# Two early input loads moved from SP's queue to ACT's queue in an attention-and-experts kernel

## The chip, the cores and the metric

The kernel runs on one core of a Trainium2 chip. The metric is device time in microseconds (us) of one execution, lower is better. Executions of one kernel here lie within about 2 us of each other; a few were 1 to 4% longer at a lower granted clock, the share of its full rate that PE was given ("slow"), and these are left out of every mean below. Each kernel also left one profile. A profile's times count from the start of its span; the span is 1.7 to 1.9 us shorter than the device time of the same run. In the profiles PE is the matmul engine, DVE, ACT and POOL are the vector, scalar and GpSimd engines, SP only issues transfers here, and a "q" behind a name marks the engine's instruction sequencer. A line of a profile begins with its start and its length in us; a bracket at its end tells how long the engine was idle before it and what ended that.

## The reference, cut to what matters

Four batches, eight heads, 768 steps, head size 48. A gated linear attention keeps a 48x48 state per head; its output goes through a mixture of four experts.

```python
f = 1.0 / (1.0 + np.exp(-f_logit))
for t in range(S):
    state = f[:, :, t, :, None] * state + np.einsum('bhd,bhe->bhde', k[:, :, t], v[:, :, t])
    y[:, :, t] = np.einsum('bhd,bhde->bhe', q[:, :, t], state)
...
p = domain_probs / (domain_probs.sum(-1, keepdims=True) + 1e-09)
for e in range(E):
    h = np.maximum(x @ w1[e], 0.0)
    out += p[:, e:e + 1] * (h @ w2[e])
```

The kernel computes the attention in six chunks of 128 steps. Only the first chunk has no expert work to hide under: until its four batches have passed attention, PE has nothing large to multiply.

## The kernel before

The order of all steps is planned in Python before anything is emitted, and each engine then runs its steps in that fixed order. The first chunk's 16 loads of 192 KB (letter: gate logits f, keys k, queries q, values v; digit: batch) are planned in this order, all from SP's queue:

```python
for i, x in enumerate("f0 k0 q0 f1 k1 q1 f2 f3 k2 q2 v0 k3 q3 v1 v2 v3".split()):
    add_load(0, x[0], int(x[1]), 1, -1000 + i)
...
def load(c, nm, b, n):
    ins[c, nm, b] = nc.sync.dma_start(out=tl(nm, c, b // 2)[:, hh(b, n), :],
                                      in_=srcs[nm][c, :, b * H:(b + n) * H, :])
```

The expert weights come through POOL's software queue, with a cast to bf16. The first of them waits for the last keys of chunk 0, and stands in POOL's order behind three key products:

```python
def load_w(i, e, which):
    w, r = (w1_sb, w1_r) if which == 1 else (w2_sb, w2_r)
    ins["w", i] = nc.gpsimd.dma_start(out=w[:, e], in_=r[e])
    if i == 0:
        after(ins["w", 0], ins[0, "k", B - 1])
```

In the first chunk, gaps of PE's plan are filled with matmuls on a constant tile, whose results nobody reads ("fillers"):

```python
for o in done:
    for _ in range(o.pad):
        nc.tensor.matmul(out=spare[:, 0:256], lhsT=busy[:, 0:128], rhs=busy, start=True, stop=True)
    o.emit(o.engine)
```

## Time and profile before

| | before |
|---|---|
| median of the first 3 runs, us | 305.67 (305.66 to 306.22) |
| span of the profile, us | 303.5 |
| PE busy | 97% |
| batch 0's logits land | 3.72 |
| last copy of chunk 0's activations ends | 22.92 |
| first expert weights land | 22.99 |
| first expert matmul starts | 23.04 |

To read it: PE is full from 23 us on, so the span is the start of the first expert matmul plus a constant. That constant is 303.5 - 23.04 = 280.5 us here. The whole question is what sets that start. Two paths end there within 0.07 us: the attention of the first chunk, ending in the copy, and the weights. The prediction shows the lines.

### The profile page before, as it was taken

Reading aid. Unit: us, or ns where it says so; the run is one execution under the profiler, and the core shown is the slowest. Engines: PE = TensorE matmul, PEld = TensorE weight load, DVE = VectorE, ACT = ScalarE, POOL = GpSimd, SP = SyncE. Lnnn points to the kernel's source line nnn. Section 1 sums busy time; section 2 is a strip of 40 time slices with the busy share of each in tenths; the row PEclk is TensorE's granted clock in tenths of the full one; section 3 lists DMA queues with packets and bytes.
Section 4 is the critical chain, followed back from the end, with each engine's and each line's share of the span. In section 5 each row is a group of like instructions: output and inputs, shape, how many; then the busy total and the mean of one; then the engine's idle time right before and its main releaser. Section 6 shows DMA issues by size and latency. Waiting matters only on the chain.

```text
span 303.5 us, 5499 instructions
## 1 busy us (share of the span) xinstructions
PE 294.5 (97%) x2104; PEld 170.5 (56%) x2135; DVE 137.8 (45%) x272; ACT 170.7 (56%) x295; POOL 95.7 (32%) x157
## 2 busy tenths in 40 slices
PE   7899999999999999999999999999999999999995
PEld 5665555567775655455555555555555555555552
DVE  6684013788853764516555344544423443201223
ACT  5767654957865444676356475345476444475430
POOL 4585200408656237423426243522432000000000
PEclk9999999999999999999999999999999999999999
DMA  7999999955993589776997877301322201100002
GB/s 156 204 185 208 208 206 190 225 90 91 215 208 82 111 165 181 170 144 120 189 178 136 213 142 151 51 13 37 92 59 51 48 14 41 73 5 2 0 0 104
DMA packets 137210, 36.08 MB, mean 119 GB/s; under 512 B 128480, under 2 KB 135648, under 8 KB 137184
## 3 DMA queue, kind: packets, MB, share of 16 engines
q1 hardware_dynamic: 131424, 29.45, 48.8%
q0 software_dynamic: 5760, 6.29, 12.5%
q8 instruction: 16, 0.26, 0.4%
q14 instruction: 10, 0.08, 0.1%
HBM read 31.51 MB, written 4.72 MB: 119 GB/s over the span
## 4 chain that ended last, share of the span: by engine, by line
PE 90%; DMA 4%; DVE 2%; POOL 1%; issue 1%; ACT 1%; DVEq 0%; ACTq 0%; POOLq 0%
PE ps_m L356 40%; PE ps_m L344 40%; DMA w_sb<-in_moe_w_dram 3%; PE ps_t L300 2%; PE ps_t L255 1%; PE ps_t L315 1%; PE ps_t L321 1%; PE ps_t L311 1%; PE ps_t L285 1%; DMA f<-in_f_logit_dram 1%; POOL qk L276 1%; PE ps_m L551 1%; DVE qk L276 1%; DVE o L363 0%; DVE AT L304 0%
## 5 line engine op out<-in xcount | busy, mean ns | idle before, releaser
L352 ACT ACTIVATE h<-ps_m 128x512 bf16<-128x512 f32 (+1 forms) x171 | 98.4, 578 | 102.7 <-PE ps_m L344 92.5
L356 PE MATMUL ps_m<-w_sb,h 128*128 128x384 bf16 x768 | 153.0, 326 | 0.2
L344 PE MATMUL ps_m<-xT,w_sb 128*128 128x512 bf16 (+1 forms) x593 | 150.4, 362 | 1.9 <-DVE o L367 0.3
L356 PEld LDWEIGHTS <-h 128*128 128x128 bf16 x768 | 72.5, 98 | 57.4
L363 DVE SCALAR_TENSOR_TENSOR o<-ps_m,pn,o 128x384 f32<-128x384 f32 x72 | 44.4, 617 | 97.2 <-PE ps_m L356 89.8
L344 PEld LDWEIGHTS <-w_sb 128*128 128x128 bf16 x624 | 59.8, 98 | 46.9 <-issue 0.7
L276 POOL TENSOR_TENSOR qk<-q,e 128x384 bf16<-128x384 f32 x19 | 22.8, 1203 | 66.7 <-ACT e L262 66.2
L304 DVE TENSOR_TENSOR AT<-ps_t,mask 128x512 bf16<-128x512 f32 x48 | 31.1, 685 | 19.3 <-PE ps_t L300 19.2
L335 POOL TENSOR_TENSOR Sf<-Sf,egs 48x192 f32<-48x192 f32 x40 | 20.4, 510 | 47.5 <-DVE Sf L328 45.5
L350 DVE TENSOR_SCALAR h<-ps_m 128x512 bf16<-128x512 f32 (+1 forms) x37 | 20.7, 573 | 22.0 <-PE ps_m L344 19.7
L276 POOL TENSOR_TENSOR qk<-k,e 128x384 bf16<-128x384 f32 x20 | 21.3, 1064 | 20.3 <-ACT e L264 13.0
L262 ACT ACTIVATE e<-ps_t 128x384 f32<-128x384 f32 x24 | 20.7, 864 | 4.6 <-PE ps_t L255 2.4
L328 DVE TENSOR_TENSOR Sf<-Sf,ps_t 48x192 f32<-48x192 f32 x40 | 14.0, 350 | 9.4 <-PE ps_t L321 8.7
L336 POOL CAST sb<-Sf 48x192 bf16<-48x192 f32 x40 | 13.6, 339 | 2.6
L551 PE MATMUL ps_m<-busy 128*128 128x256 bf16 x71 | 13.1, 332 | 1.3 <-DVE busy L140 1.3
L365 ACT ACTIVATE o<-ps_m,pn 128x384 f32<-128x384 f32 x20 | 11.6, 581 | 3.9 <-PE ps_m L356 3.1
L264 ACT ACTIVATE e<-ps_t 128x384 f32<-128x384 f32 x24 | 13.0, 541 | 0.0
L218 DVE CAST yb<-ps_t 128x384 bf16<-128x384 f32 x16 | 8.9, 556 | 7.3 <-PE ps_t L315 6.3
L247 ACT ACTIVATE ex<-f 128x768 f32<-128x768 f32 (+1 forms) x14 | 10.5, 747 | 3.0 <-DMA f<-in_f_logit_dram 3.0
L315 PE MATMUL ps_t<-vb,AT 128*128 128x48 bf16 x192 | 11.4, 184 | 0.7 <-DVE vb L218 0.7
L315 PEld LDWEIGHTS <-AT 128*128 128x128 bf16 x192 | 9.8, 97 | 2.8 <-issue 0.9
L251 ACT ACTIVATE gp<-ex 128x768 bf16<-128x768 f32 (+1 forms) x14 | 10.5, 751 | 0.4
(50 smaller groups left out, 142.6 us busy)
## 6 DMA issues: line engine op xcount, KB each, us to landing
w_sb<-in_moe_w_dram POOLq DMA_DIRECT2D x8, 768.0 KB, 18.6
out_dram<-o SPq DMA_DIRECT2D x24, 192.0 KB, 1.9
f<-in_f_logit_dram SPq DMA_DIRECT2D x10, 384.0 KB, 4.2
k<-in_k_dram SPq DMA_DIRECT2D x10, 384.0 KB, 5.3
q<-in_q_dram SPq DMA_DIRECT2D x10, 384.0 KB, 5.3
v<-in_v_dram SPq DMA_DIRECT2D x10, 384.0 KB, 5.5
f<-in_f_logit_dram SPq DMA_DIRECT2D x4, 192.0 KB, 3.8
k<-in_k_dram SPq DMA_DIRECT2D x4, 192.0 KB, 3.9
```

Source lines behind the costliest of these rows:

```text
L262: nc.scalar.activation(out=e[:, 0].rearrange("t (d h) -> t h d", d=D), in_=cs[:, 0:HD].rearrange("t (i r d) -> t r i d", r=2, d=D), func=A ...
L276: engines[eng].tensor_tensor(out=tl("qk", c, b)[:, j, :, 0:D].rearrange("t (i r) d -> t i r d", r=2), in0=tl("qk"[j], c, b // 2)[:, hh(b), ...
L304: nc.vector.tensor_tensor(out=tl("AT", c, b)[:, r].rearrange("s i t -> s (i t)"), in0=tl("A", c, b, r).rearrange("s i t -> s (i t)"), in1= ...
L315: nc.tensor.matmul(out=y[:, h * D:(h + 1) * D], lhsT=AT[:, r, i, :], rhs=vb[:, h, :], start=(c == 0), stop=True, skip_group_check=True)
L328: nc.vector.tensor_tensor(out=Sf[rows, b], in0=Sf[rows, b], in1=KV[rows, :, r, :], op=ALU.add)
L335: nc.gpsimd.tensor_tensor(out=Sf[rows, b], in0=Sf[rows, b], in1=eg, op=ALU.mult)
L344: nc.tensor.matmul(out=tl("hp", c, e, fc, n0)[:, n0:n1], lhsT=w1_sb[:, e, kk, fc * 128:(fc + 1) * 128], rhs=tl("xT", c)[:, kk, n0:n1], sta ...
L350: nc.vector.tensor_relu(out=dst, in_=src)
L352: nc.scalar.activation(out=dst, in_=src, func=AF.Relu)
L356: nc.tensor.matmul(out=tl("op", c, e, nt)[:, 0:Din], lhsT=tl("h", c, e)[:, fc, nt * T:(nt + 1) * T], rhs=w2_sb[:, e, fc, :], start=(fc == ...
L363: nc.vector.scalar_tensor_tensor(out=o, in0=op, scalar=pe, in1=o, op0=ALU.mult, op1=ALU.add)
L551: nc.tensor.matmul(out=spare[:, 0:256], lhsT=busy[:, 0:128], rhs=busy, start=True, stop=True)
```

## The change

The intent is to have two sequencers start the first loads, so that they get going sooner: batch 0's keys and batch 1's logits are issued by ACT, which waits for its first data anyway.

```diff
     def load(c, nm, b, n):
-        ins[c, nm, b] = nc.sync.dma_start(out=tl(nm, c, b // 2)[:, hh(b, n), :],
+        ins[c, nm, b] = (nc.scalar if (c, nm, b) in ((0, "k", 0), (0, "f", 1)) else nc.sync).dma_start(out=tl(nm, c, b // 2)[:, hh(b, n), :],
                                           in_=srcs[nm][c, :, b * H:(b + n) * H, :])
```

PE, DVE and POOL keep their instruction order. SP has two issues fewer; ACT has two more, behind its table load and ahead of the first exponential.

## The prediction

> **What bounds the kernel now.** I read the page from the top, then the chain of waits in order of time, then the timeline of the first 24 us and the stretches of one us for the DMA. On the page I looked at busy time first:
>
> ```profile
> span 303.5 us, 5499 instructions
> PE 294.5 (97%) x2104; PEld 170.5 (56%) x2135; DVE 137.8 (45%) x272; ACT 170.7 (56%) x295; POOL 95.7 (32%) x157
> ```
>
> PE is busy for 97% of the span, and the stretches of ten us show 9.6 to 10.0 us of PE in nearly each after 30 us. So from the first large matmul on, the time is PE's own work, and a change that touches only the first microseconds moves the end by as much as it moves that first matmul. PE's count in the first 23 us includes filler matmuls on the tile "busy", so there being busy proves nothing; the chain of waits says what counts (start, length, what):
>
> ```profile
> 0.81 2.91 DMA f<-in_f_logit_dram
> 3.74 0.53 ACT ex L247
> 4.29 0.53 ACT gp L251
> 4.87 0.48 PE ps_t L255
> 5.34 0.28 PE ps_t L258 x4
> 5.63 2.58 PE ps_m L551 x12
> 8.21 0.43 PE ps_t L285 x4
> 8.63 0.32 PE ps_t L255
> ...
> 13.60 1.31 POOL qk L276
> 14.91 8.08 DMA w_sb<-in_moe_w_dram
> ...
> 23.04 0.39 PE ps_m L344
> ```
>
> The head is thus: batch 0's gate logits land at 0.81 + 2.91 = 3.72 us, gates, cumulative sum, a fixed run of fillers, batch 1's sum, products, then the first expert weights, which land at 14.91 + 8.08 = 22.99, and the first expert matmul at 23.04. The timeline (start, length, engine, and in brackets the wait) shows a second path that ends in the same tenth of a microsecond, the last of the four transposed activations:
>
> ```profile
> 22.44 0.48 ACT L216 COPY xT<-ps_t 128x384 bf16<-128x384 bf16 x1 [0.74 <-PE ps_t L340]
> 23.03 0.55 PEld L344 LDWEIGHTS <-w_sb 128*128 128x128 bf16 x4 [0.36 <-DMA w_sb<-in_moe_w_dram]
> ```
>
> The copy ends at 22.92, the weights land at 22.99. The change can gain only if both come earlier; it loses if either comes later.
>
> The change concerns the loads, so I looked at their issues on SP's queue and at the DMA engines (last two columns of the stretches: busy share of the 16 engines, GB/s):
>
> ```profile
> 0.81 0.45 SPq L222 DMA_DIRECT2D f<-in_f_logit_dram  x1
> 1.31 0.57 SPq L222 DMA_DIRECT2D k<-in_k_dram  x1
> 1.92 0.80 SPq L222 DMA_DIRECT2D q<-in_q_dram  x1
> 2.76 0.71 SPq L222 DMA_DIRECT2D f<-in_f_logit_dram  x1
> ...
> 1.00:2.00 1.00, 0.74 (x4) 0.56 (x5) 1.00 (x7) 1.00 (x1) 0.79 (x5) 1.00 0.02 5
> 2.00:3.00 1.00, 1.00 (x7) 0.69 (x6) 0.89 (x7) 0.09 (x1) 0.93 (x4) 1.00 0.95 186
> 3.00:4.00 1.00, 1.00 (x6) 0.69 (x5) 0.89 (x2) 0.26 (x1) 0.44 (x1) 1.00 1.11 221
> ```
>
> Bytes flow from 2.0 us, and from then on the engines are full (share about 1, some 190 to 230 GB/s in most stretches up to 17 us). One load is 192 KB, so at about 205 GB/s it costs some 0.95 us. The landings, issue plus time to landing, agree: batch 0's logits 3.7, its keys 4.5, its queries 5.6, batch 1's logits 6.4, its keys 7.5 us, steps of 0.8 to 1.15 us. SP's sequencer is not what limits the loads after the very first; its issues stretch to 0.7 to 1.5 us because the engines behind them are full.
>
> **What the Trainium skill says.** (1) "DMA: Bandwidth & Descriptors", section "Issuing engines are not separate DMA queues": transfers started by several engines run on the same 16 DMA engines and interleave; starting them from more engines saves only the sequencer's time for the start. The trace agrees as far as one queue can show it: 16 full engines from 2.0 us. (2) The same page, section "Queues, rings and completion order": SP and ACT each have a ring on each DMA engine, and an engine takes turns between rings packet by packet. Before, only SP's ring held these loads, so no run yet shows the turns. (3) "Perfetto Trace Analysis", section "DVE / Act Engine Instruction": the sequencer is free for the next instruction once it has pushed one to the wait queue; so the table load on ACT (0.80 to 2.08 us here) need not hold back the issues behind it. This trace has no issue on ACT and can't confirm it. (4) The same page, section "DMA Instruction — HWDGE": descriptor generation is locked for one issue at a time. The first, undisturbed, issue took 0.45 us on SP here.
>
> **The change part by part.** *Removed from SP:* two issues, 0.57 and 0.71 us. Batch 0's queries, batch 1's keys and all later loads can be issued 0.6, then up to 1.3 us earlier. Bytes and DMA engines stay the same, and these were full, so all loads together land no earlier: gain 0. Nothing on the chain waits for those later loads either (batch 2's and 3's logits have landed when ACT comes to them at 10.40 and 11.39 with no wait shown).
>
> *Added to ACT:* two issues of 0.45 to 0.8 us, ahead of the first exponential in ACT's order. ACT stands idle from 2.08 to 3.74, "1.65" in its timeline, waiting for the logits. If the issues run beside the table load they end near 2.5; if they start behind it at 2.08, near 3.4. Either way before 3.74: cost 0.
>
> *Moved in the rings:* this is the part that counts. Before, batch 0's logits had the DMA engines alone: data about 2.0 to 3.0 us, plus 0.7 to the landing. Now batch 0's keys stand in a second ring. Case A, ACT issues during the table load, from about 0.9 us: with the generator locked in turn the keys start 0.45 us behind the logits; the logits move 0.45 us of their 0.95 us alone and the other 0.5 at half speed in 1.0 us: landing 0.5 us later, about 4.2. If the two generators run freely or ACT comes first, up to 0.9 us later, about 4.6. Case B, ACT issues only from 2.08: the keys' bytes come near 3.3 us, when the logits are through: 0. But then batch 1's logits, second in ACT's ring and sharing with SP's, end after four loads' work from about 3.3 us, so near 7.3 + 0.7 = 8.0 at worst, against 6.4 before. They were needed at 6.79 with some 0.4 to 0.6 us to spare (their gate ended at 7.86; PE started on it at 8.43 behind fillers and transposes). Cost 0 to 0.6, say 0.2.
>
> Nothing between 3.7 and 22.9 us takes up a delay of the first logits: PE is in program order, and the 12 fillers and everything behind them move as a block; POOL, DVE and ACT wait for each other and not for a clock. So the last copy of the activations moves from 22.92 to 22.92 + d, and the first expert matmul from 23.04 to about 23.04 + d - 0.07. The weights themselves should still land near 23.0: POOL issues them d later, but the DMA engines have input loads to move until 18 us, and all bytes up to the end of the first weights stay the same.
>
> Sum: case A (7 in 10) about +0.55, case B (3 in 10) about +0.15: +0.4 us. 305.67 + 0.4 = **306.1 us**.
>
> **Rivals.** *The loads flow sooner and the head gets shorter.* For it: SP is rid of 1.28 us, and the first weights wait in POOL's order behind products that need loaded keys. Against it: share about 1 from 2.0 us on, and no load but the first ended a wait on the chain. It could gain at most the 0.07 us between the two paths without moving both; I give it 0.1 to 0.3 us of gain at best, 305.4.
>
> *PE's own speed in the head.* A filler of 128x256 takes 3.17 / 14 = 0.23 us at the start and 0.71 / 5 = 0.14 us near 21 us; the row of granted clock is full throughout. PE runs slower until about 10.5 us. A longer idle gap before its first real matmul (0.44 us now, about 1 us in case A) may put the step to the fast rate later. Each us of that would cost perhaps 0.3 us more on the chain; time 306.5 to 307.
>
> *The transfer is hidden anyway.* If ACT's ring gets its turn only after SP's first load is through, nothing moves and the time is 305.7 within the scatter of the three runs (305.66 to 306.22).
>
> *Delay absorbed later.* PE waits 0.29 us near 70 us for a product on DVE; what released that is itself behind PE, so I expect 0 to 0.2 us back.
>
> **Range and chances.** Gain 0.3 and absorbed delay give the lower end, 305.4; full sharing (+0.9) with a little of the slower PE gives the upper end, 306.8. Two per cent is 6.1 us, more than any term here and nearly half of what the head from the logits' landing to the weights' issue takes (11.2 us). So within 2% with 0.985; faster by that 0.005; slower 0.01, for a disturbed order I don't see.
>
> **What the changed profile would show.** ACT's queue has two issues, near 0.9 (case A) or 2.1 us (case B). The chain's first piece ends at 4.2 to 4.6 us in case A instead of 3.72; in case B batch 1's exponential shows a wait for its logits. The DMA's share stays about 1 from 2.0 us. The 12 fillers, the later sums and the last copy of the activations move by one amount, and the first expert matmul then waits for that copy instead of the weights, which still land near 23.0. From there to the end the length is unchanged, some 280 us. The prediction is wrong if the logits land no later yet the time rises, if the weights land more than 0.3 us away from 23.0, or if the stretch behind 23 us changes length.

## The result, and the profile after

Median 305.6 us (304.81 to 316.58, six runs, one of them slow) against 305.67. Ratios here are the mean time of one kernel's fast runs over that of the other's fast runs of the same rounds, so they are not quite the ratio of the medians: 0.9992, with a 95% interval of 0.997 to 1.0013.

The profile after has a span of 304.3 us, 0.8 more than before. First the issues, in the timeline of the changed kernel (start, length, queue; lines of other work between them are left out):

```profile
0.80 0.45 SPq L222 DMA_DIRECT2D f<-in_f_logit_dram  x1
0.83 0.48 ACTq L222 DMA_DIRECT2D k<-in_k_dram  x1
1.31 0.57 SPq L222 DMA_DIRECT2D q<-in_q_dram  x1
1.34 0.70 ACTq L222 DMA_DIRECT2D f<-in_f_logit_dram  x1
...
4.41 0.52 ACT L247 ACTIVATE ex<-f 128x384 f32<-128x384 f32 x1 [2.33 <-DMA f<-in_f_logit_dram]
```

ACT issues its first load 0.03 us after SP's, during its own table load (0.80 to 2.08 us). The exponential that needs batch 0's logits waits 2.33 us for them instead of 1.65. Now the chain of waits of the changed kernel in order of time:

```profile
0.80 3.58 DMA f<-in_f_logit_dram
...
4.41 0.53 ACT ex L247
...
5.54 0.48 PE ps_t L255
...
6.30 2.58 PE ps_m L551 x12
8.88 0.43 PE ps_t L285 x4
...
14.28 1.31 POOL qk L276
15.59 8.21 DMA w_sb<-in_moe_w_dram
23.81 0.05 issue
23.85 0.39 PE ps_m L344
```

Set it against the chain in the prediction: the logits land at 4.38 instead of 3.72 (+0.66), the fillers start at 6.30 instead of 5.63 (+0.67), the last key product ahead of the weights at 14.28 instead of 13.60 (+0.68), the weights are issued at 15.59 instead of 14.91 (+0.68). The head moved as one block. The last step did not keep to that: the weights landed 0.81 us later, at 23.80, behind the last copy of the activations, which ends at 23.61:

```profile
23.13 0.48 ACT L216 COPY xT<-ps_t 128x384 bf16<-128x384 bf16 x1 [0.74 <-PE ps_t L340]
23.85 1.47 PE L344 MATMUL ps_m<-xT,w_sb 128*128 128x512 bf16 x5 [0.21 <-DMA w_sb<-in_moe_w_dram]
```

The DMA engines are at least as full as before. These are stretches of one us (the last two columns are the engines' busy share and GB/s):

```profile
1.00:2.00 1.00, 0.75 (x4) 0.56 (x5) 1.00 (x7) 1.00 (x1) 0.79 (x5) 1.00 0.03 7
2.00:3.00 1.00, 1.00 (x7) 0.69 (x6) 0.89 (x7) 0.09 (x1) 0.93 (x4) 1.00 0.96 176
3.00:4.00 1.00, 1.00 (x6) 0.69 (x5) 0.89 (x2) 0.00 (x0) 0.44 (x1) 1.00 1.28 258
```

Two queues moved no more bytes between 1 and 3 us (183 KB against 191 before), only in another order. From 3 to 6 us they moved about a tenth more (242 GB/s against 218), but from 1 to 12 us it is 192 against 187, and kernels of one queue reach 192 as well. So the profile shows a loss of 0.8 us, and the timed runs show none. The experiments ask whether the later logits really cost time, and why the clock does not show it.

### The profile page after: what moved, and what is told of

Same layout as the page of the kernel before. It is cut to its first block, busy times and chain, and to the rows that moved or that the text cites. A ratio compares the mean times of both kernels' runs of the same rounds, so it can differ in the third digit from the quotient of the medians.

```text
span 304.3 us, 5499 instructions
## 1 busy us (share of the span) xinstructions
PE 294.4 (97%) x2104; PEld 170.1 (56%) x2135; DVE 137.9 (45%) x272; ACT 170.7 (56%) x295; POOL 95.7 (31%) x157
## 4 chain that ended last, share of the span: by engine, by line
PE 90%; DMA 4%; DVE 2%; issue 1%; POOL 1%; ACT 1%; DVEq 0%; ACTq 0%; POOLq 0%
PE ps_m L356 40%; PE ps_m L344 40%; DMA w_sb<-in_moe_w_dram 3%; PE ps_t L300 2%; PE ps_t L255 1%; PE ps_t L315 1%; PE ps_t L321 1%; PE ps_t L285 1%; DMA f<-in_f_logit_dram 1%; PE ps_t L311 1%; PE ps_m L551 1%; DVE qk L276 1%; POOL qk L276 0%; DVE o L363 0%; DVE AT L304 0%
## 5 line engine op out<-in xcount | busy, mean ns | idle before, releaser
L276 POOL TENSOR_TENSOR qk<-q,e 128x384 bf16<-128x384 f32 x19 | 22.8, 1203 | 66.7 <-ACT e L262 66.2
```

Of the source, the lines that this page charges most:

```text
L276: engines[eng].tensor_tensor(out=tl("qk", c, b)[:, j, :, 0:D].rearrange("t (i r) d -> t i r d", r=2), in0=tl("qk"[j], c, b // 2)[:, hh(b), ...
```

## The experiments

Twelve runs in three sets. Each set had its own 10 or 11 fast runs of the kernel before, with means of 305.50, 305.68 and 305.27 us; with the six first runs that is 37 runs, mean 305.50, standard deviation 0.53. All profiles in one table (us):

| kernel | logits land | last copy ends | weights land | first expert matmul | span |
|---|---|---|---|---|---|
| before | 3.72 | 22.92 | 22.99 | 23.04 | 303.5 |
| changed | 4.38 | 23.61 | 23.80 | 23.85 | 304.3 |
| a1_again (changed) | 4.26 | 23.47 | 22.9 | 23.52 | 303.9 |
| a2_keys_first | 4.82 | 23.41 | 24.81 | 24.86 | 305.2 |
| a4_logits_fourth | 6.34 | 25.19 | 24.2 | 25.24 | 305.7 |
| b2_k_only_held | 3.57 | 22.57 | 22.87 | 22.92 | 303.4 |
| b1_k_only | 4.29 | 23.13 | 24.0 | 24.09 | 304.8 |
| c1_late_fill | 3.77 | 23.93 | 22.4 | 23.98 | 304.3 |
| c2_late_fill_two_queues | 4.23 | 24.81 | 22.8 | 24.86 | 305.5 |
| e1_fewer_fillers | 3.74 | 22.57 | 23.4 | 23.43 | 304.2 |
| e1_again | 3.70 | 22.52 | 22.76 | 22.80 | 303.2 |
| e2_fewer_fillers_two_queues | 4.33 | 22.99 | 23.3 | 23.30 | 304.0 |
| c1_again | 3.59 | 24.09 | 23.5 | 24.14 | 304.5 |
| c2_again | 4.21 | 24.53 | 22.4 | 24.58 | 305.3 |

In every row the first expert matmul starts right behind the later of the two columns before it. (Weights given to one decimal are issue plus the profile's rounded time to landing.)

### First set: is it the later logits, and what is it worth?

**a1_again**: the changed kernel, no edit.

> The changed kernel once more, to tell the size of its effect from the scatter. Theory 1 (the later landing of batch 0's logits is carried one to one to the end): batch 0's logits land 3.5 to 3.6 us after their issue, the first expert matmul starts near 23.85 us, and the timed ratio is 1.002 to 1.003 (+0.6 to +0.9 us). Theory 2 (the end is not tied to the head so tightly; the +0.8 us of the one profile is scatter from run to run): ratio 0.999 to 1.001.

Measured: ratio 0.999 (0.9972 to 1.0007), mean 305.21 us. The landing (4.26 us, 3.45 behind its issue) was nearly as Theory 1 said. The first expert matmul at 23.52 was later than before by 0.48 us, not by the expected 0.8, and the ratio showed no loss. By the ratio alone, Theory 2 holds. With the first set of timed runs, the changed kernel has 11 fast runs with a mean of 305.29, 0.21 below the 37 runs of before, with a standard error of 0.15 from the spread of the runs.

**a2_keys_first**: one queue, the keys ahead of the logits.

```diff
-    done = P.run()
+    done = P.run(); j = next(i for i, o in enumerate(done) if o.name == "ld k0.0"); i = next(i for i, o in enumerate(done) if o.name == "ld f0.0"); done.insert(j, done.pop(i))
```

> One queue only, as before the change, but batch 0's keys are issued on SP ahead of batch 0's logits. Theory 1: logits land near 4.4 to 4.6 us (0.7 to 0.9 later), fillers, sums, last copy and first expert matmul move by the same amount, ratio 1.002 to 1.003: the same loss as the changed kernel without a second queue. Theory 2: ratio within 0.001 of 1. Rival 3 (the second queue itself costs something): first expert matmul near 23.1 and ratio 1.000 here, unlike the changed kernel.

Measured: ratio 1.0022 (1.0004 to 1.004), as Theory 1 had it, from a landing 1.1 us later instead of the expected 0.7 to 0.9. So this order costs time with one queue as well, and Rival 3 is not needed for a loss. That the later logits are the cost is not shown by it, because in its profile, of the slowest of the six runs, the weights came last:

```profile
22.93 0.48 ACT L216 COPY xT<-ps_t 128x384 bf16<-128x384 bf16 x1 [0.73 <-PE ps_t L340]
24.86 1.47 PE L344 MATMUL ps_m<-xT,w_sb 128*128 128x512 bf16 x5 [1.42 <-DMA w_sb<-in_moe_w_dram]
```

The activations were ready at 23.41 and PE waited another 1.4 us for the weights, which took 9.4 us from issue to landing; before the change it was 8.1, in a1_again 7.5. The same 768 KB, in the same place of the program.

**a4_logits_fourth**: the same edit with "ld f0.1" as the mark, so that batch 0's logits are issued fourth.

> The suspected cause made large: batch 0's logits are issued fourth on SP, behind batch 0's keys and queries and batch 1's logits. Theory 1: they land near 6.4 us (+2.7), the first expert matmul starts near 25.6 to 25.8, the end moves by +2.6 to +2.9 us, ratio 1.0085 to 1.0095. Theory 2: later waits take up most of it, ratio under 1.004.

Measured: ratio 1.0066 (1.0048 to 1.0085), mean 307.52 against 305.50. The logits landed 2.6 us later and the end moved by 2.0 us. Theory 2's "under 1.004" is out, and Theory 1's full size (1.0085 to 1.0095) was not reached. The last copy moved by 2.27 us only: from landing to copy it took 18.85 us instead of 19.20. And by their mean span of 303.78, less 280.45, the runs of the kernel before start their expert matmuls not at 23.04 but near 23.3 on average; with the constants seen it can be 23.0 to 23.5. That suggests that many of them wait for something else already.

**b2_k_only_held**: only the keys go to ACT's queue, and ACT holds them for a POOL memset that ends near 2.3 us.

```diff
-(nc.scalar if (c, nm, b) in ((0, "k", 0), (0, "f", 1)) else nc.sync)
+(nc.scalar if (c, nm, b) == (0, "k", 0) else nc.sync)
...
-    nc.gpsimd.memset(ones, 1.0)
+    ones_set = nc.gpsimd.memset(ones, 1.0)
...
-        if (c, nm, b) == (1, "f", 0):
-            after(ins[c, nm, b], ins["w", 5])
+        if (c, nm, b) in ((0, "k", 0), (1, "f", 0)):
+            after(ins[c, nm, b], ones_set if c == 0 else ins["w", 5])
```

> Only batch 0's keys go to ACT's queue, and they wait there for a memset on POOL that ends near 2.3 us, so that their bytes come when the logits are through. Theory 1: logits land at 3.7 us as before the change, the whole head is where it was (first expert matmul near 23.05), ratio 0.999 to 1.001, although a second queue is in use. Rival 3 (the second queue itself costs): logits or the first expert matmul late by 0.3 us or more.

Measured: the logits landed at 3.57 us. The ratio, 1.0018, has an interval of 0.9979 to 1.0056 because one of its six runs took 309.07 us without being counted as slow; the other five average 305.47. (Its granted clock was 0.994, but a run of the kernel before took 305.40 at the same clock, so that does not explain it.) So the landing speaks clearly against Rival 3 and the time is inconclusive alone.

### Second set: take the weights out of the way

**b1_k_only** is b2 without the hold, one look. The edit is the first change of b2's diff.

> Only batch 0's keys on ACT's queue, not held back. If the two rings share the DMA engines from the start: batch 0's logits land at 4.2 to 4.4 us (3.6 to 3.7 when the same load was held until 2.3 us) and the last copy of the activations ends near 23.4 to 23.6 us. If not: landing at 3.7.

Measured: landing at 4.29 us; the one execution took 306.48 us. ACT's timelines behind its table load, of b2_k_only_held and, in the second fence, of b1_k_only:

```profile
2.30 0.42 ACTq L222 DMA_DIRECT2D k<-in_k_dram  x1
3.58 0.52 ACT L247 ACTIVATE ex<-f 128x384 f32<-128x384 f32 x1 [1.50 <-DMA f<-in_f_logit_dram]
```

```profile
4.30 0.52 ACT L247 ACTIVATE ex<-f 128x384 f32<-128x384 f32 x1 [2.22 <-DMA f<-in_f_logit_dram]
```

The same load on the same second queue delays the logits by 0.7 us when it is issued beside them, and not at all when issued 1.5 us later. It is the time of the issue that matters, not the queue. The last copy came at 23.13, earlier than the 23.4 to 23.6 expected; the weights, at 24.0, set the start.

**c1_late_fill** and **c2_late_fill_two_queues**: 16 more fillers ahead of the last activation transpose, in the kernel before and in the changed one.

```diff
-        for _ in range(o.pad):
+        for _ in range(o.pad + 16 * (o.name == "xt 0.3")):
```

> The kernel before with 16 more filler matmuls on PE ahead of the last activation transpose, so that the last copy of the activations ends about 1.8 us later and the landing of the first expert weights (22.9 to 24.8 us in the profiles so far) no longer sets the start of the expert matmuls. Theory A (the landing of the first weights scatters by more than a microsecond from run to run, is what most runs of the kernel before wait for, and hides a delay of the head): first expert matmul near 24.6 us, span near 305.0, ratio 1.003 to 1.005, runs within 0.7 us of each other. Theory B (the scatter is elsewhere, behind the start of the expert matmuls): the runs scatter as before, by 1.5 us or more.

> The same 16 fillers in the changed kernel; the pair with the run before it shows the change with the weights' landing out of the way. Theory A: batch 0's logits land near 4.3 us, the first expert matmul starts 0.5 to 0.65 us later than in the pair's other kernel, and the mean time is 0.4 to 0.7 us higher. Theory B (the two queues win back elsewhere what the later logits cost): the two means differ by less than 0.2 us.

Measured: c1 306.34 us (four fast runs), c2 306.79 us (six), ratios 1.0018 and 1.0033 to the kernel before; the difference of the pair is 0.45 us. In both the copy now sets the start; first c1, then c2:

```profile
23.45 0.48 ACT L216 COPY xT<-ps_t 128x384 bf16<-128x384 bf16 x1 [2.20 <-PE ps_t L340]
...
23.98 1.46 PE L344 MATMUL ps_m<-xT,w_sb 128*128 128x512 bf16 x5
```

```profile
24.33 0.48 ACT L216 COPY xT<-ps_t 128x384 bf16<-128x384 bf16 x1 [2.20 <-PE ps_t L340]
...
24.86 0.81 PE L344 MATMUL ps_m<-xT,w_sb 128*128 128x512 bf16 x2
```

The matmul lines have no wait for the weights. c1's four fast runs lie within 0.6 us of each other, where ten runs of the kernel before in the same set lie between 304.82 and 307.03. With the repeat below, nine runs have a standard deviation of 0.24 us, against 0.53 for the 37. That is what Theory A said. Its size for c1 was too large (first expert matmul near 24.6 and a ratio of at least 1.003 expected, 23.98 and 1.0018 measured), and the profiles show why the copies of the pair differ by 0.88 us although the logits differ by 0.46. These are the first fillers behind batch 0's sum, c1 first:

```profile
5.41 1.47 PE L551 MATMUL ps_m<-busy 128*128 128x256 bf16 x12
```

```profile
6.00 2.72 PE L551 MATMUL ps_m<-busy 128*128 128x256 bf16 x12
```

The same 12 matmuls took 1.47 us in one run and 2.72 us in the other: PE went to its fast rate near 5.5 us in c1 and near 9.5 us in c2, by the lengths of its matmuls. The Trainium skill, "TensorE: Matmul & The Clock Gate", Part 1, has it that PE starts at half rate and is let to full rate by a monitor that watches activity in windows of about 3.4 us which run free of the program. The two lengths agree with half and full rate; no run shows the windows themselves. The profile's row of granted clock does not show this step, it reads 1.00 from the start.

**e1_fewer_fillers**: the kernel before with 8 fillers in place of 12 ahead of the first product transpose.

```diff
-        for _ in range(o.pad):
+        for _ in range(o.pad + -4 * (o.name == "tpq 0.0")):
```

> The kernel before with 4 fewer fillers ahead of the first product transpose (8 in place of 12). If the head moves as one block with the fillers on it: that transpose starts near 7.4 to 7.5 us in place of 8.0, the last copy of the activations ends 0.5 to 0.75 us earlier, near 22.2 to 22.4. Theory A then has the time follow the weights' landing: gain 0.1 to 0.5 us, ratio 0.9985 to 0.9995. If the first weights' issue also moves up with the block, up to 0.6 us, ratio 0.998.

Measured: the first transpose came at 7.49 us instead of 8.00 and the last copy ended at 22.57 instead of 22.92, less than expected. Ratio 0.9971 (0.9951 to 0.9991), a larger gain than expected. In its profile the copy is ready and PE waits for the weights, the reverse of c1:

```profile
22.09 0.48 ACT L216 COPY xT<-ps_t 128x384 bf16<-128x384 bf16 x1 [0.74 <-PE ps_t L340]
...
23.43 1.25 PE L344 MATMUL ps_m<-xT,w_sb 128*128 128x512 bf16 x4 [0.84 <-DMA w_sb<-in_moe_w_dram]
```

### Third set: repeat the pairs

The changed kernel's mean of 305.29 us left a suspicion that two queues win something back, for instance by bringing the weights earlier. If so, it must show where the weights set the start.

> The kernel before with 8 fillers in place of 12 once more, as partner of the next run: last copy of the activations near 22.6 us, so that the landing of the first weights sets the start of the expert matmuls in nearly every run. Mean near 305.1 us, 0.4 to 0.7 us below the kernel before.

> The changed kernel with the same 8 fillers: both kernels of the pair wait for the first weights in most runs. Theory A (the change only delays the head, and the scatter of the weights hides that): mean equal to the pair's other kernel or up to 0.4 us higher. Theory B (with two queues the input loads are through earlier and the first weights land earlier): mean 0.2 us or more below the other kernel of the pair.

e2 is the changed kernel with e1's edit. Measured: e1_again 305.19 us (ratio 0.9999, 0.9982 to 1.0015), e2 305.55 us (ratio 1.0008, 0.9992 to 1.0024). Against all 12 runs of e1 (mean 305.14), e2 is 0.41 us higher, with a standard error of 0.17 (against its own set alone 0.35, with 0.19). Theory B falls in this pair: the two queues do not win. And e1's gain of the second set did not come again; over both sets it is 0.36 us below the kernel before, 0.1%, so it is no version worth the name.

> The kernel before with 16 late fillers once more (two of its six runs were slow): mean near 306.3 us, spans 304.2 to 305.1.

> The changed kernel with 16 late fillers once more: if the later logits cost what the traces show whenever the weights don't set the start, the mean is again 0.3 to 0.65 us above the pair's other kernel; if the first pair's difference of 0.45 us was scatter, under 0.2 us.

Measured: c1_again 306.20 us, c2_again 307.02 us; difference 0.82 us, a little over the expected 0.65. Both sets together: 306.26 (9 runs) and 306.91 (12 runs), a difference of 0.65 us with a standard error of 0.14. So in this pair, where the copy sets the start, the change costs about 0.65 us or 0.2%. Not all of that is shown to come from the later logits. In the profiles the first expert matmul of c2 comes 0.88 and 0.44 us later than that of c1, but the spans differ by 1.2 and 0.8: the rest, 0.3 to 0.4 us, arises near 110 us, where both profiles of c2 (c2_late_fill_two_queues first) wait for a transfer and those of c1 don't:

```profile
110.02 0.40 PE L300 MATMUL ps_t<-QK 48*128 48x128 bf16 x8 [0.23 <-DMA QK<-qk]
```

```profile
109.84 0.40 PE L300 MATMUL ps_t<-QK 48*128 48x128 bf16 x8 [0.33 <-DMA QK<-qk]
```

None of the other 12 profiles has this wait, the changed kernel's own included, and no run tells what causes it.

## Why the prediction was right or wrong

**The time** (306.1, range 305.4 to 306.8): the median of 305.6 lies in the range. The predicted rise of 0.4 us is not in the timed runs. The hit is in part luck: the range, 1.4 us wide, also holds no change at all, and the loss that was predicted is there in the profile and not in the mean of the runs. (A slip without effect: 6.1 us is not nearly half of 11.2 but a little more than half.)

**The added issues on ACT cost nothing themselves, and come during the table load (case A):** right. They ran from 0.83 to 2.04 us, and ACT's first exponential came at 4.41.

**The removed issues on SP gain nothing:** right. Share about 1 or more from 2 us on, no more bytes by 3 us, and the tenth more from 3 to 6 us ended no wait on the chain.

**The logits land 0.5 us later if the generator serves the issues in turn, up to 0.9 if freely:** right in size, 0.5 to 0.7 in the profiles (4.21 to 4.38 us). The issues did not go in turn: they began 0.03 us apart and took 0.45 and 0.48 us, which is the second sub-case, and its 0.9 was too much. b1 and b2 show the cause: the same load beside the logits or 1.5 us behind them.

**Everything up to the last copy moves as a block:** right in the one profile after (all steps +0.66 to +0.69), and less exact from run to run. a4 gave 2.27 us for 2.62, and the step of PE to its fast rate moves the copy by some tenths of a microsecond. The prediction had that step as a rival, for a longer gap on PE. In the six profiles with a load on ACT beside the logits the step came near 9 us or later; in four of the six with the logits at 3.8 us or earlier it came before 7, in the kernel before near 10. That fits the rival, but twelve profiles don't prove it.

**"The weights themselves should still land near 23.0":** this is the step that was mis-sized. As an average it held: in the five profiles with one queue and the logits first (before, c1, c1_again, e1, e1_again) they landed at 23.0 on average, in the five of the changed loads (changed, a1, c2, c2_again, e2) at 23.1. As a fixed time it did not: 22.4 to 23.8 in these ten, and 24.8 in a2. In the profile after it was 23.80, 0.8 us off, which by the prediction's own sign of being wrong (more than 0.3 us) makes that step wrong; and the first expert matmul waited for the weights, not for the copy as forecast. The prediction read one profile, in which copy and weights ended within 0.07 us, and passed the copy's whole delay on to the start. The runs speak for a kernel before that often waits for the weights: its copy ended at 22.92 in the profile, yet by the spans its mean start is near 23.3. That is an estimate, since timed runs leave no trace of the wait. A delay of the copy counts only from where the weights end.

**After 23 us nothing changes:** right for the changed kernel itself (280.5 us before, 280.5 and 280.4 after). It does not hold for every variant: the 280.6 to 280.8 us of b1, e1, e2, c2 and c2_again against 280.3 to 280.5 in the others. PE waits 0.15 and 0.23 us near 55 us in b1 and e1, and for the transfer near 110 us in both c2. "Delay absorbed later" played no part; in these profiles delay was added.

**What stays open.** By the two pairs the changed kernel should be about 0.3 to 0.6 us slower than the kernel before, less what the weights hide. Its 11 runs have a mean 0.21 us lower. Hiding alone can bring the difference to near zero and not below it, and with a standard error of 0.15 zero is not excluded. But six of the 11 runs have spans of 303.1 to 303.3, a start near 22.7 to 22.9, which needs a copy earlier than any profile of the changed kernel itself shows. Whether the logits landed sooner in those runs or PE reached its fast rate sooner can't be told, since only profiled runs leave a trace. Nor is it shown what makes the weights take 7.0 to 9.4 us, or what adds the waits near 55 and 110 us.

## What to carry to other kernels

Before giving early loads to a second queue, see whether the DMA engines or the sequencer limit them. Where the engines are full from the first byte, as here, expect a second queue to change mainly who comes first, and give the transfer that heads the longest chain the engines to itself: hold the others back for its length (b2: landing at 3.57 us instead of 4.29). And before passing a delay on to the end, ask from several runs, not one profile, what the last wait really is; a pair of variants that takes the other wait out of the way shows a cost of 0.2% that the plain comparison can't. Then compare the pair's profiles to the end of the span: part of such a difference can arise far behind the place that was changed.

## What the Trainium skill lacked or had wrong

- "DMA: Bandwidth & Descriptors", section "Issuing engines are not separate DMA queues", is right that the second issuer only saves issue time. It says that the transfers interleave, but lacks what that costs the load that was alone before: here 0.5 to 0.7 us on a landing at 3.7 us.
- "Perfetto Trace Analysis", section "DMA Instruction — HWDGE", has descriptor generation locked to one issue at a time. Two issues from SP and ACT that began 0.03 us apart took 0.45 and 0.48 us, against 0.45 us for SP's alone: no such wait shows at this size.
- "TensorE: Matmul & The Clock Gate", Part 1, gives about half a microsecond of scatter for the step to the fast rate. In these programs, whose PE work has short gaps, it came anywhere between about 5.5 and 10 us, 4 to 9 us behind the first filler at 1.25: 12 equal matmuls took 1.47 or 2.72 us.
- No page that I read gives the scatter of one load through POOL's software queue: 768 KB took 7.0 to 9.4 us from issue to landing in 14 profiles, with input loads running beside it.
